# A two-stage attention and gated MLP kernel on one core: its beginning scheduled anew

## Chip, core and metric

One core of one Trainium2 chip runs one program. The metric is the device time of one execution in microseconds (us). The kernel before takes 796.01 us, the median of three runs (795.81 to 797.61).

## What is computed

```python
def _attn_ref(q, k, v, p):
    # sm_attn(a, b, c) = softmax(a @ b.T / 8) @ c, for each batch and head
    p_packed = sm_attn(p, k, v)
    return sm_attn(q, p_packed, p_packed)

def _moe_ref(x, w_gate, w_val, w_out, rms_g):
    rms = np.sqrt(np.mean(x * x, axis=-1, keepdims=True) + 1e-06)
    xn = x / rms * rms_g
    g = xn @ w_gate
    silu = g * (1.0 / (1.0 + np.exp(-g)))
    return silu * (xn @ w_val) @ w_out
```

There are 8 batches, 8 heads, 576 positions, 64 columns a head and 32 packed rows. x is the attention output laid out as 4608 tokens by 512; w_gate and w_val are 512 by 1536, w_out is 1536 by 512, all float32.

## The kernel before

**Two kinds of work.** Per batch b, `stage1` turns k, v and p into 32 packed rows a head (`pk_0x`, `pk_1x`, then transposed into `pts_0x`, ScalarE L831), and `packed_weights` multiplies these rows with the weights w_gate and w_val (L898, six column blocks c, eight products each), so that the MLP's first product is taken directly from the second attention's probabilities. Per unit u of 384 tokens, `query` and `attention` make the probabilities: scores (L1030), softmax (L1054 to L1064), transposition (L932), a product that gives the norm (L1099), its squares (L1107), the norm itself on GpSimd (L1124 to L1138), scaled probabilities (L1152), transposed again into `aTu`. `mlp` then runs 24 products of six multiplications (L1197, 12 column tiles ft for the gate and the value), each pair followed by `gated` (SiLU on ScalarE L1231, product with the value L1234, split into a high and a low half L1239 and L1245 into `hall`), and three output products of 36 multiplications each (L1222) whose results `store` writes out. There are 12 units. Everything is exact to about float32 by splitting into two float16 halves.

**The beginning.** Batch 0 and 1 and units 0 and 1 are done in a float32 way with transpositions on TensorE. In the beginning the weights are also made ready. `gv_piece(i)` loads one of 12 pieces of w_gate and w_val (1 MB each, alternately) into a raw room, turns it into a usable float32 form in `to_f32` (ScalarE L404, GpSimd L409, VectorE L411), squares it (ScalarE L459) and sums the squares over the rows on TensorE (L470). From each pair of pieces come scales: VectorE L481, then the small operations L345 to L350, L484, L486; GpSimd multiplies the w_val half by the ratio of the two scales (L489) and makes `gv_sc` and `wo_sc` (L492 to L494). `wo_piece(i)` loads and turns the six pieces of w_out in the same way (L404, L409, L411, squares L521); `wo_scale` waits for all six and makes one common scale (L538); `wo_split(i)` scales a piece (L554 on ScalarE or L557 on VectorE), writes its high half (ScalarE L559) and its low half (GpSimd L565). The raw rooms 0 to 3 lie in `ring`, 4 to 6 in `wo`, 7 and 8 in `hall`; a room is loaded again only once the piece in it has been turned, and `hall` can take results of `gated` only once the w_out pieces have left its rooms.

**What sets the order.** `Plan` is a list scheduler that runs while the program is built. Each job is a generator (a chain) that yields the engine, an estimated cost and the rooms or marks that it needs. `Plan.run` takes the step that can start first by the estimates; within a window (`CHOICE`, per engine) the step with the smallest rank (`RANK`) goes first. All engines then run the resulting fixed orders. All loads, stores and DMA transposes go through SyncE's one queue in that order. ScalarE needs one table for Exp and another for SiLU, and loads a table (ACT_TABLE_LOAD) whenever it goes from the one to the other.

Of the kernel before, what the change touches and what calls it, by code (L numbers as in the profile page):

```python
# [9 lines left out]
F32 = mybir.dt.float32  # L10
# [8 lines left out]
P = 128  # L19
# [14 lines left out]
LATENCY = {PE: 0.293, ACT: 0.16, EXP: 0.16, SILU: 0.16, DVE: 0.14, POOL: 0.1}  # L34
# [20 lines left out]
DVE_COST = (0.08, 1.04e-3)  # L55
# [17 lines left out]

class Plan:
# [36 lines left out]
    def go(self, chain, value=None):  # L111
        self.now, self.sent, self.chain = chain[2], chain[3], chain
        try:
            chain[4] = chain[0].send(value)
        except StopIteration:
            self.chains.remove(chain)
            return
        chain[2] = max(chain[2], self.now) if chain[4] is not None else self.now

    def settle(self):  # L120

        again = True
        while again:
            again = False
            for chain in sorted(self.chains, key=lambda c: (c[2], c[1])):
                ask = chain[4]
                if ask is None:
                    self.go(chain)
                elif isinstance(ask, Room):
# [15 lines left out]

    def start(self, chain):
        kind, _, *at = chain[4]
        e = ENGINE[kind]
        ready = at[0] if at and at[0] is not None else chain[3] if e == chain[5] and e in ("pe", "sp") else chain[2]
        if e == "pe" and chain[1] != NEVER:  # L150
            ready += SLACK[self.warm]
        return max(self.free[e], ready)

    def run(self):
        while self.chains:
            self.settle()
            steps = [c for c in self.chains if c[4] is not None and c[4][0] in ENGINE]
# [1175 lines left out]
```

## Time and profile before

| what | value |
|---|---|
| median of three runs | 796.01 us |
| the profiled execution, its own time | 796.5 us |
| its span, first to last instruction | 794.5 us |
| mean granted TensorE clock over the span | 0.967 |
| TensorE busy | 737.0 us (93%) |
| VectorE busy | 483.9 us (61%) |
| ScalarE busy | 472.2 us (59%) |
| GpSimd busy | 101.4 us (13%) |
| chain that ended last: TensorE's share | 78% |

Times within the trace count from the span's start. PE is TensorE, ACT ScalarE, DVE VectorE, POOL GpSimd, and SPq is SyncE's queue of DMA issues. PEclk is the granted TensorE clock as a share of 2.4 GHz: 0.50 is the level of 1.2 GHz, 1.00 that of 2.4 GHz. A matmul's end is modelled, so a busy PE is not a PE at its peak. A wait is named with the instruction that ended it.

### The profile page before, as it was taken

The numbers are of one execution on the slowest core, as the hardware profiler recorded it, in microseconds if no ns is written. First come the engines' busy times: TensorE is split into PE (matmuls) and PEld (weight loads), VectorE is DVE, ScalarE is ACT, GpSimd is POOL, SyncE is SP. The second block draws the span as 40 slices with busy tenths as digits, with TensorE's granted clock in tenths as the row PEclk, the third lists the DMA queues.
The fourth block names the chain that finished last, engine by engine and source line by source line (L and its number), as shares of the span: only waits on it lengthen the run. The fifth ranks groups of instructions, "written<-read, shape, count | busy, mean of one in ns | idle before, by whom it ended". The sixth has DMA issues, their size and how long they took to land.

```text
span 794.5 us, 17852 instructions
## 1 busy us (share of the span) xinstructions
PE 737.0 (93%) x7502; PEld 425.1 (54%) x7502; DVE 483.9 (61%) x985; ACT 472.2 (59%) x839; POOL 101.4 (13%) x144
## 2 busy tenths in 40 slices
PE   3676977799999999999999999999999999999998
PEld 2452543467544455478454555477455455676553
DVE  1768868487478447667578376476677465473341
ACT  1858877567658448658767457368677366271230
POOL 1666516101000000000001001000010000000000
PEclk9677989899999999999999999999999999999999
DMA  9994414343632732561636341734337212300001
GB/s 262 386 314 118 157 56 104 73 86 87 143 72 51 177 97 68 102 138 27 157 78 125 80 116 24 176 83 107 90 65 149 68 35 61 93 18 24 27 1 41
DMA packets 135504, 82.16 MB, mean 103 GB/s; under 512 B 98432, under 2 KB 123008, under 8 KB 135424
## 3 DMA queue, kind: packets, MB, share of 16 engines
q1 hardware_dynamic: 135424, 81.02, 42.0%
q8 instruction: 59, 0.97, 0.5%
q14 instruction: 21, 0.17, 0.1%
HBM read 47.97 MB, written 9.44 MB: 72 GB/s over the span
## 4 chain that ended last, share of the span: by engine, by line
PE 78%; ACT 7%; DVE 6%; DMA 5%; SPq 2%; issue 2%; POOL 1%; ACTq 0%; DVEq 0%; POOLq 0%
PE pm_2x L1222 11%; PE pm_1x L1222 10%; PE pm_2x L1197 8%; PE pm_1x L1197 8%; PE pm_0x L1222 8%; PE pm_3x L1197 7%; PE pm_0x L1197 7%; PE pm_3x L1222 6%; DMA hall<-in_moe_w_gate_dram 2%; PE pm_3x L898 2%; SPq L442 2%; PE quad L1037 1%; DMA big_3x<-in_k_dram 1%; PE pm_0x L898 1%; PE quad L793 1%
## 5 line engine op out<-in xcount | busy, mean ns | idle before, releaser
L1197 PEld LDWEIGHTS <-ring 128*128 128x128 f16 x2304 | 205.7, 98 | 107.0 <-issue 35.9
L1222 PEld LDWEIGHTS <-hall 128*128 128x128 f16 x1296 | 123.8, 99 | 153.0 <-issue 15.4
L1222 PE MATMUL pm_2x<-wo,hall 128*128 128x512 f16 x396 | 90.1, 379 | 0.0
L1222 PE MATMUL pm_1x<-wo,hall 128*128 128x512 f16 x360 | 81.8, 380 | 0.0
L1222 PE MATMUL pm_0x<-wo,hall 128*128 128x512 f16 x324 | 75.2, 382 | 3.3 <-POOL wo L565 3.3
L1239 ACT CAST hall<-t_1x 128x384 f16<-128x384 f32 x72 | 36.8, 510 | 34.9 <-DVE t_1x L1234 34.3
L1245 DVE TENSOR_TENSOR hall<-t_1x,hall 128x384 f16<-128x384 f32 x72 | 41.7, 579 | 17.2 <-ACT hall L1239 14.8
L1245 DVE TENSOR_TENSOR hall<-t_0x,hall 128x384 f16<-128x384 f32 x72 | 41.6, 578 | 14.9 <-ACT hall L1239 14.6
L1222 PE MATMUL pm_3x<-wo,hall 128*128 128x512 f16 x216 | 49.2, 383 | 0.0
L1239 ACT CAST hall<-t_0x 128x384 f16<-128x384 f32 x72 | 36.6, 508 | 17.1 <-DVE t_0x L1234 15.9
L1197 PE MATMUL pm_2x<-aTu_0x,ring 128*128 128x192 f16 (+1 forms) x324 | 45.6, 285 | 1.0 <-DVE ring L363 0.6
L1197 PE MATMUL pm_1x<-aTu_1x,ring 128*128 128x192 f16 (+1 forms) x324 | 45.8, 285 | 0.2 <-ACT t_0x L1231 0.2
L1197 PE MATMUL pm_3x<-aTu_1x,ring 128*128 128x192 f16 (+1 forms) x288 | 41.2, 286 | 3.1 <-DVE ring L363 1.7
L1197 PE MATMUL pm_1x<-aTu_0x,ring 128*128 128x192 f16 (+1 forms) x312 | 43.5, 283 | 0.2 <-ACT t_0x L1231 0.2
L1197 PE MATMUL pm_2x<-aTu_1x,ring 128*128 128x192 f16 (+1 forms) x288 | 41.3, 286 | 0.9 <-ACT hall L1239 0.7
L1197 PE MATMUL pm_0x<-aTu_0x,ring 128*128 128x384 f16 (+1 forms) x270 | 40.2, 291 | 0.7 <-ACT t_1x L1231 0.3
L1197 PE MATMUL pm_3x<-aTu_0x,ring 128*128 128x384 f16 (+1 forms) x246 | 37.6, 296 | 0.6 <-ACT t_1x L1231 0.5
L1197 PE MATMUL pm_0x<-aTu_1x,ring 128*128 128x384 f16 (+1 forms) x252 | 36.6, 288 | 0.0
L363 DVE SCALAR_TENSOR_TENSOR ring<-pm_3x,pw_sc,ring 128x512 f16<-128x512 f32 x31 | 23.1, 745 | 9.1 <-ACT ring L361 9.0
L361 ACT ACTIVATE ring<-pm_3x,pw_sc 128x512 f16<-128x512 f32 x31 | 21.1, 682 | 7.3 <-PE pm_0x L898 5.7
L1107 ACT ACTIVATE quad<-quad 128x512 f32<-128x512 f32 x36 | 21.1, 587 | 6.7 <-PE quad L1099 6.2
L363 DVE SCALAR_TENSOR_TENSOR ring<-pm_0x,pw_sc,ring 128x512 f16<-128x512 f32 x27 | 20.1, 746 | 7.8 <-ACT ring L361 7.4
(832 smaller groups left out, 1254.9 us busy)
## 6 DMA issues: line engine op xcount, KB each, us to landing
out_dram<-o_1x SPq DMA_DIRECT2D x18, 256.0 KB, 2.2
out_dram<-o_0x SPq DMA_DIRECT2D x18, 256.0 KB, 2.5
big_2x<-in_k_dram SPq DMA_DIRECT2D x6, 576.0 KB, 7.5
wo<-in_moe_w_gate_dram SPq DMA_DIRECT2D x3, 1024.0 KB, 14.3
wo<-in_moe_w_val_dram SPq DMA_DIRECT2D x3, 1024.0 KB, 10.8
ring<-in_moe_w_out_dram SPq DMA_DIRECT2D x3, 1024.0 KB, 5.5
hall<-in_moe_w_out_dram SPq DMA_DIRECT2D x3, 1024.0 KB, 5.0
big_0x<-in_v_dram SPq DMA_DIRECT2D x4, 576.0 KB, 6.3
```

Of the source, the lines that this page charges most:

```text
L361: nc.scalar.activation(hi, x, AF.Copy, scale=s)
L363: nc.vector.scalar_tensor_tensor(lo, x, s, hi, ALU.mult, ALU.subtract)
L442: nc.sync.dma_start(raw.rearrange("p k n e -> p k (n e)"), (w_gate, w_val)[n][:, 4 * c * P : 4 * (c + 1) * P].rearrange("(kt p) f -> p kt ...
L793: nc.tensor.matmul(pp[32 * j : 32 * j + 32, :D], a1T[:, c, 32 * j : 32 * j + 32], vf[:, j, cv, :], start=(c == 0), stop=(c == NCK - 1),)
L898: nc.tensor.matmul(ps[e][32 * j : 32 * j + 32, :], pg[h, j, :], wgv[h, c, j, :, :].rearrange("p w f -> p (w f)"), start=True, stop=True,)
L1037: nc.tensor.matmul(ps2[o : o + n, i, :, pi, :], qT[:, lq, i, pi, o : o + n], packs[b][3][:, lp, pi, :, :], start=(j == 0), stop=(j == 2),)
L1107: nc.scalar.activation(x, x, AF.Square, scale=2.0**-14, accum_out=ss[:, i : i + 1])
L1197: nc.tensor.matmul(psi[:, :, o : o + n], pw[:, g, lw, w, f * P : (f + 1) * P], aT[:, :, la, g, o : o + n], start=(j == 0), stop=(j == 5),)
L1222: nc.tensor.matmul(po, hall[:, ft, lh, ts], wo[:, ft, lw, :], start=(n == 0), stop=(n == 3 * NFT - 1))
L1239: nc.scalar.copy(hall[:, ft, 0, :], t)
L1245: nc.vector.tensor_tensor(hall[:, ft, 1, :], t, hall[:, ft, 0, :], ALU.subtract)
```

## The change

The scheduler gets two sets of constants: one (index 0) up to the point where unit 1's attention is planned to its end, one (index 1) after that. Ranks in the first set can depend on the number of the batch, unit or piece (`LATER`). Estimated costs change a little. A filler that could put dummy multiplications into idle time of TensorE is written, but its constants leave it out of the program. Then the steps themselves:

- the product of the w_val half with the scale ratio goes from GpSimd to ScalarE (column blocks 0 and 5 by the string `VAL_BY`'s letters A) and VectorE (D);
- the sums of squares go to another PSUM room, and each piece has its own maximum (12 short reductions in place of six longer ones);
- p of a batch is loaded ahead of its k; k of batch 1 waits for the issue of piece 9 in place of piece 11; w_out's pieces no longer wait for each other's issue;
- w_out's pieces use rooms 7, 8, 3, 8, 3, 8 in place of 8, 3, 8, 3, 8, 3;
- one more w_out scaling and one low half go to VectorE, some copies change between ScalarE and VectorE, and two low halves of unit 0 go to GpSimd.

```diff
-CHOICE = {'pe': 0.1, 'act': 0.335, 'dve': 0.324, 'pool': 0.378, 'sp': 0.437}
+CHOICE = ({'pe': 0.0, 'act': 0.281, 'dve': 0.275, 'pool': 0.352, 'sp': 0.398}, {'pe': 0.2, 'act': 0.36, 'dve': 0.338, 'pool': 0.208, 'sp': 0.269})
+IN_TURN = range(12)
+FILL = (0.6, 0.0, 0.0)
...
-RANK = {"scales": 0.1, "gated": 0.44, "pw_evict": 0.3, "store": 0.4, "attention": 0.63, "stage1": 0.6, "keys": 0.67, "v": 0.66, "query": 0.79, "pw": 0.8, "g": 0.9, "w": 1.0, "wo": 1.5, "wo_split": 1.65}
+RANK = ({"mlp": 1e9, "scales": 0.31, "gated": 0, "pw_evict": 0.39, "store": 0, "attention": 0.37, "stage1": 0.87, "keys": 0.49, "v": 0.21, "query": 0.79, "pw": 1.18, "g": 1.02, "w": 1.33, "wo": 1.34, "wo_split": 1.33}, {"mlp": 1e9, "scales": 0, "gated": 0.44, "pw_evict": 0.11, "store": 0.25, "attention": 0.71, "stage1": 0.6, "keys": 0.51, "v": 1.08, "query": 0.88, "pw": 1.56, "g": 1.6, "w": 1.13, "wo": 1.95, "wo_split": 1.52})
+LATER = {"attention": 0.08, "stage1": -0.24, "keys": 0.0, "query": 0.0, "pw": 0.17, "w": 0.04, "wo": 0.0, "wo_split": 0.04}
...
-WO_AT = (8, 3, 8, 3, 8, 3)
+WO_AT = (7, 8, 3, 8, 3, 8)
...
+VAL_BY = "DADDDA"
...
-WO_BY = "ADADAD"
-WO_LO = "PPPPPP"
-H_LO = "DDDDDDDDDDDD"
+WO_BY = "ADADDD"
+WO_LO = "PDPPPP"
+KEYS_AFTER = 9
+KEYS_BY = "ADAAAAADAADA"
+QUERY_BY = "ADDDAD"
+H_LO = "DDDPDDDDDDDP"
...
     def gv_piece(i):
...
-        if i:
-            yield "load", i - 1
+        if i and i in IN_TURN:
+            yield "issued", i - 1
...
-            pns[c] = yield Room("pm")
+            pn = yield Room("pa")
...
+        yield DVE, 0.4
+        nc.vector.tensor_reduce(mx[:, n : n + 1], pn[:, 2 * P :], AX.X, ALU.max)
...
-        yield POOL, pool(1024)
-        nc.gpsimd.tensor_scalar_mul(x, x, mx[:, 0:1])
+        if VAL_BY[c] == "A":
+            yield ACT, act(1024)
+            nc.scalar.activation(x, x, AF.Copy, scale=mx[:, 0:1])
+        elif VAL_BY[c] == "D":
+            yield DVE, 0.75
+            nc.vector.tensor_scalar_mul(x, x, mx[:, 0:1])
...
     def wo_piece(i):
...
-        yield ("load", 2 * NFC + i - 1)
+        if 2 * NFC + i in IN_TURN:
+            yield ("issued", 2 * NFC + i - 1)
...
     def keysets(b):
...
-        if b == 1:
-            yield ("load", 2 * NFC - 1)
+        if b == 1 and KEYS_AFTER:
+            yield ("issued", KEYS_AFTER)
...
+        pf = yield Room("pf")
+        for j in range(4):
+            yield LOAD, 16384
+            nc.sync.dma_start(pf[32 * j : 32 * j + 32], p[b, 2 * j : 2 * j + 2].rearrange("g r d -> r g d"))
+        t_p = plan.now
         kf0 = [None] * 2
...
     def gated(u, ft, pss, done):
...
-        if u == 0 and 8 in WO_AT and ft >= 5:
-            yield ("raw", 8, RAW_AT.count(8) + WO_AT.count(8))
+        if u == 0:
+
+            for k in (7,) if ft < 5 else (7, 8) if ft == 5 else (8,):
+                if k in WO_AT:
+                    yield ("raw", k, RAW_AT.count(k) + WO_AT.count(k))
```

What the scheduler makes of it is shown at three places. Line numbers of the change are those of its own file: L449 there is L404 of before, L507 is L459, L591 is L521, L857 is L766, L875 is L784, L1323 is L1231, L1338 is L1239, L1062 is L972, L1121 is L1030, L919 is L828, L988 is L898, L511 is L470, L700 is L610.

The first place is SyncE's queue behind the loads of q for unit 1. Before, k and p of batch 1 come next, then the fifth w_val piece:

```order
L959 DMA big_5x<-in_q_dram 64x8x192 x2
L576 DMA big_3x<-in_k_dram 96x4x384
L576 DMA big_0x<-in_k_dram 96x4x384
L599 DMA pf_0x<-in_p_dram 32x2x64 x4
L442 DMA wo_77<-in_moe_w_val_dram 128x4x512
L506 DMA ring<-in_moe_w_out_dram 128x2x1024
```

With the change:

```order
L1049 DMA big_5x<-in_q_dram 64x8x192 x2
L576 DMA ring<-in_moe_w_out_dram 128x2x1024
L489 DMA wo_79<-in_moe_w_val_dram 128x4x512
L682 DMA pf_0x<-in_p_dram 32x2x64 x4
L664 DMA big_3x<-in_k_dram 96x4x384
L664 DMA big_0x<-in_k_dram 96x4x384
```

A piece of w_out and the fifth w_val piece now stand ahead of p and k of batch 1, and p ahead of k. (At the queue's start p of batch 0 likewise stands ahead of its k.)

The second place is TensorE between the transposition of batch 0's packed rows (L828, with the change L919) and the scores of unit 0 (L1030, with the change L1121). Before, transpositions of unit 1's q (L972), one piece's sums (L470) and the transposition of batch 1's p (L610) stand between:

```order
L828 MATMUL quad<-ident_66,pk_1x 64x128
L972 MATMUL pm_0x<-ident_66,big_5x 64x128 x8
L972 MATMUL pm_1x<-ident_66,big_5x 64x128 x8
...
L470 MATMUL pm_2x<-o_1x,onesb 128x256
L610 MATMUL pm_3x<-ident_66,pf_0x 64x128 x4
L972 MATMUL pm_0x<-ident_66,big_5x 64x128 x8
L1030 MATMUL quad<-pb_0_85,big_4x 128x2x32 x12
```

With the change:

```order
L908 MATMUL quad<-tiny_0x,ones 128x1 x2
L919 MATMUL quad<-ident_66,pk_0x 64x128
L919 MATMUL quad<-ident_66,pk_1x 64x128
L1121 MATMUL quad<-pb_0_87,big_4x 128x2x32 x12
L988 MATMUL pm_1x<-wgv,pg_0x 32x512
```

The scores now follow at once, and what stood between comes after the first block of packed weights (L988).

The third place is ScalarE around its first SiLU. Before, the first softmax of batch 1 (L766) is followed by the table for SiLU, and the second comes in the middle of unit 0's SiLUs, behind a table load of its own; these rows are those around that second softmax:

```order
L1231 ACTIVATE t_0x<-pm_0x,usc_0x 128x384
L404 ACTIVATE wo_77<-hall 128x1024
L766 ACT_TABLE_LOAD
L766 ACTIVATE a_0x,tiny_43x<-quad,tiny_42x,qk_74 128x576
L1239 CAST hall<-t_1x 128x384
...
L521 ACTIVATE o_0x,wo_ss<-wo_77 128x1024
L1231 ACT_TABLE_LOAD
L1231 ACTIVATE t_1x<-pm_3x,usc_0x 128x384
```

With the change, before the first SiLU:

```order
L857 ACTIVATE a_0x,tiny_36x<-quad,tiny_35x,qk_76 128x576
L591 ACTIVATE o_1x,wo_ss<-wo_79 128x1024
L875 COPY a1T_0x<-quad 96x768
L591 ACTIVATE o_0x,wo_ss<-wo_79 128x1024
L552 ACTIVATE wgv<-wgv,tiny_33x 128x4x256
L896 ACTIVATE junk_0x,tiny_31x<-pk_2x 128x64
L449 ACTIVATE wo_79<-hall 128x1024
L857 ACTIVATE a_0x,tiny_43x<-quad,tiny_42x,qk_76 128x576
L1323 ACT_TABLE_LOAD
L1323 ACTIVATE t_0x<-pm_0x,usc_0x 128x384
```

Between the copy of unit 0's scaled probabilities (L940, with the change L1030) and the first SiLU stand now both softmaxes of batch 1, four conversions and three squares of w_out pieces, one square of a w_val piece and one ratio product (L552). No table load is left among unit 0's SiLUs.

## Rows read from the trace of the kernel before

**Rows 1.** Busy time by stretch: stretch, its length, busy time of each engine (instructions), PEclk, DMA

```profile
0.00:45.95 45.95, 23.30 (x252) 15.84 (x253) 21.79 (x52) 22.68 (x32) 23.08 (x32) 0.77 1.02 313
45.95:82.00 36.05, 25.73 (x293) 16.02 (x293) 27.06 (x53) 24.99 (x39) 24.27 (x26) 0.78 0.62 197
...
88.66:122.15 33.49, 28.94 (x258) 16.48 (x256) 23.70 (x49) 28.77 (x51) 6.25 (x5) 0.90 0.29 95
122.15:143.76 21.61, 12.82 (x112) 5.04 (x112) 17.38 (x24) 15.15 (x23) 13.23 (x8) 0.94 0.37 94
143.76:165.00 21.24, 21.24 (x266) 11.70 (x267) 9.71 (x25) 10.65 (x20) 1.96 (x5) 0.90 0.37 69
165.00:740.00 575.00, 567.89 (x6000) 330.75 (x5999) 360.56 (x748) 352.37 (x644) 27.90 (x62) 1.00 0.41 90
```

**Rows 2.** Timeline of the first 46 us: start, length, engine, line, what [idle before <-what ended it]

```profile
2.93 2.12 SPq L599 DMA_DIRECT2D pf_0x<-in_p_dram  x4
...
13.76 1.13 PE L610 MATMUL pm_0x<-ident,pf_0x 128*64 128x128 f32 x8 [13.76 <-DMA pf_0x<-in_p_dram]
...
15.64 1.98 PE L972 MATMUL pm_1x<-ident,wgv 128*64 128x128 f32 x16
...
22.14 0.72 PE L738 MATMUL quad<-wgv,pT_0x 64*32 64x288 f32 x16
...
45.95 0.37 ACT L831 ACTIVATE pts_0x<-quad,tiny_20x 128x128 f32<-128x128 f32 x1 [0.67 <-PE quad L828]
```

**Rows 3.** The chain of waits, its first piece

```profile
2.20 10.53 DMA big_3x<-in_k_dram
```

**Rows 4.** Instructions by line and form up to 145 us, ScalarE: busy us, mean ns | idle before

```profile
L404 ACT ACTIVATE wgv<-wo 128x1024 f32<-128x1024 f32 x6 | 6.8, 1132 | 2.1 <-DMA wo<-in_moe_w_val_dram 2.1
L459 ACT ACTIVATE o_0x<-wgv 128x1024 bf16<-128x1024 f32 x6 | 6.3, 1057 | 3.5 <-DVE wgv L411 3.5
L1231 ACT ACT_TABLE_LOAD x2 | 2.6, 1283 | 0.0
```

**Rows 5.** Timeline, 45 to 85 us: GpSimd's ratio, TensorE, the last w_val piece, the scaled probabilities

```profile
45.63 3.90 POOL L489 TENSOR_SCALAR wgv<-wgv,tiny_17x 128x1024 f32<-128x1024 f32 x1
...
51.30 0.66 PE L610 MATMUL pm_3x<-ident,pf_0x 128*64 128x128 f32 x8 [1.45 <-DMA pf_0x<-in_p_dram]
...
52.77 2.89 PE L1030 MATMUL quad<-pb,big_4x 128*128 128x64 f32 x24
...
61.47 1.15 POOL L409 TENSOR_SCALAR wo<-wo 128x1024 uint32<-128x1024 uint8 x1 [1.66 <-DMA wo<-in_moe_w_val_dram]
...
76.76 1.31 ACT L1152 ACTIVATE e_0x<-e_0x,trio_3x 128x256 f32<-128x256 f32 x3 [0.20 <-POOL trio_3x L1138]
...
84.84 1.14 PE L1197 MATMUL pm_0x<-aTu_0x,ring 128*128 128x384 f16 x6 [0.21 <-DVE ring L363]
```

**Rows 6.** Timeline, VectorE's scaling of a w_out piece, alone and beside GpSimd's low halves

```profile
120.59 0.75 DVE L557 TENSOR_SCALAR big_2x<-wo,wo_sc 128x1024 f32<-128x1024 f32 x1
...
133.08 2.62 DVE L557 TENSOR_SCALAR big_0x<-wo,wo_sc 128x1024 f32<-128x1024 f32 x1
```

**Rows 7.** Timeline, ScalarE and TensorE from the first SiLU on

```profile
88.66 0.58 ACT L1231 ACTIVATE t_0x<-pm_0x,usc_0x 128x384 f32<-128x384 f32 x1
...
122.15 0.56 ACT L1231 ACTIVATE t_1x<-pm_3x,usc_0x 128x384 f32<-128x384 f32 x1
...
135.74 1.04 ACT L559 CAST wo<-big_0x 128x1024 f16<-128x1024 f32 x1 [4.19 <-DVE big_0x L557]
...
143.76 1.51 PE L932 MATMUL quad<-ident,e_0x 128*128 128x128 f32 x6 [4.13 <-DVE e_0x L1064]
...
146.34 3.47 PE L1222 MATMUL pm_3x<-wo,hall 128*128 128x512 f16 x12
```

**Rows 8.** The chain of waits, one output product of 36 multiplications

```profile
320.47 7.77 PE pm_1x L1222 x36
```

**Rows 9.** DMA issues up to 160 us: KB each, median us to landing

```profile
hall<-in_moe_w_out_dram SPq DMA_DIRECT2D x3, 1024.0 KB, 5.0
```

**Rows 10.** Timeline, one later attention: its DMA transposition and its first use

```profile
304.90 1.43 SPq L1077 DMA_TRANSPOSE aT_0x<-hl_0x  x1
...
309.08 0.21 PE L1099 MATMUL quad<-pav_0x,aT_0x 32*64 32x64 f16 x1
```

More of the change, by code (lines that the diff above doesn't have):

```diff
@@ L71, with __init__ @@
     pass
+class Chain:
+    def __init__(self, gen, key, t):
+        self.gen, self.key = gen, key
+        self.end = self.sent = t
+        self.since = 0.0
+        self.ask = self.engine = None
 class Plan:
     def __init__(self):
+        self.rooms = {}
         self.now = self.sent = 0.0
@@ L152, in start, with fill @@
-        return max(self.free[e], ready)
-    def run(self):
+        if at and at[0] is not None:
+            base = at[0]
+        else:
+            base = chain.sent if e == chain.engine and e in ("pe", "sp") else chain.end
+        ready = max(base, chain.since)
+        t = float(ready)
+        if e == "pe" and chain.key[0] != "mlp":
+            t += SLACK[self.stage]
+        return max(self.free[e], t), ready
+    def fill(self, until, matmul):
+        begin = self.free["pe"]
+        n = int(FILL[1] * (until - begin) / 0.11)
+        for name in ("pa", "psc", "pm"):
+            spare = [r for r in self.rooms[name] if r[0] <= begin]
+            if spare:
+                break
+        if until - begin < FILL[0] or until > FILL[2] or not spare or not n:
+            return
+        self.rooms[name].remove(spare[0])
+        for _ in range(n):
+            matmul(spare[0][1])
+        self.free["pe"] += 0.11 * n
+        self.rooms[name].append((self.free["pe"], spare[0][1]))
@@ L162, in run @@
-            for n, c in enumerate(steps):
-                t = self.start(c)
-                t -= AGE * max(0.0, t - c[2])
-                if c[4][0] in (EXP, SILU) and c[4][0] != self.table:
-                    t += TABLE
-                starts[n] = t
-            first = min(starts, key=lambda n: (starts[n], steps[n][1]))
-            e = ENGINE[steps[first][4][0]]
-            near = [n for n in starts if ENGINE[steps[n][4][0]] == e and starts[n] <= starts[first] + CHOICE[e]]
-            chain = steps[min(near, key=lambda n: (steps[n][1], starts[n]))]
@@ L172, in run @@
-            t, (kind, cost, *_) = self.start(chain), chain[4]
-            e = ENGINE[kind]
+            starts = []
+            for c in steps:
+                t, ready = self.start(c)
+                t -= AGE[self.stage] * max(0.0, t - ready)
+                if c.ask[0] in (EXP, SILU) and c.ask[0] != self.table:
+                    t += TABLE
+                starts.append((t, self.precedence(c), c))
+            first = min(starts, key=lambda s: s[:2])
+            e = ENGINE[first[2].ask[0]]
@@ L174, in run @@
+            window = CHOICE[self.stage][e]
+            chain = min(
+                (s for s in starts if ENGINE[s[2].ask[0]] == e and s[0] <= first[0] + window), key=lambda s: (s[1], s[0])
+            )[2]
+            t, ready = self.start(chain)
+            kind, cost, *_ = chain.ask
+            if e == "pe":
+                self.fill(t, matmul)
+                t = max(t, self.free["pe"])
             if kind == LOAD:
```

303 lines of the change are left out of this document (170 added, 133 removed).

## The prediction

> **What bounds the kernel now.** I read the busy time by stretch first, then the timeline of the beginning, then the chain of waits. From 165 to 740 us TensorE is busy for 567.9 of 575 us at a granted clock of 1.00 [rows 1]: that part is TensorE's own work, and the change leaves the number of multiplications as it is. Up to 143.76 us it is otherwise: no engine is full, and TensorE waits. It does nothing until 13.76, because p lands last [rows 2]; it makes its first MLP product at 84.84 [rows 5]; from 122.15 to 143.76 it is busy for 12.8 of 21.6 us [rows 1]. From 143.76 on it hardly stops. So the time is, to a few us, the moment at which TensorE becomes dense, plus a remainder that stays. The engine to follow up to there is ScalarE: 25.0 of 36.1 us, then 28.8 of 33.5 us, the fullest of all in the MLP's first unit [rows 1].
>
> The profiled execution took 796.5 us (span 794.5 and 2.0 around it), 0.5 above the median of 796.0.
>
> **The change, milestone by milestone.**
>
> *Batch 0's packed rows (ScalarE L831, 45.95 before).* The second half of k lands at 2.20 + 10.53 = 12.73 [rows 3]; p, whose four issues come behind it (2.93 to 5.05), lands at 13.76, and TensorE's queue begins with p [rows 2]. With p first, p waits for nothing and k, held back by 64 KB, lands near 13.0. Then k's transpositions end near 15; the first group of unit 0's q stands next, can start as now when q is there (15.64 [rows 2]) and takes 1.1 to 2 us; the scores L738 follow near 16.8 in place of 22.14: 5.3 earlier, because the other q groups now stand behind them. From L738 to L831 it is 23.8 us. Twelve conversions and squares stand on ScalarE between the steps of this chain, ten with the change, 1.13 or 1.06 each [rows 4]: 2.2 less, and 0.8 for waits on pieces that have landed by then. So 16.8 + 20.8 = 37.6; ends 36 and 41.
>
> *First MLP product (84.84 before).* From L831 to the copy of unit 0's final probabilities ScalarE works 25.0 of 36.1 us [rows 1]; in the new order a conversion, a square and a ratio product are added (1.13 + 1.06 + 1.13, the last priced by L404, same shape and engine [rows 4]): 28.3 us. Two waits go: unit 0's scores stood behind batch 1's p, which landed at 51.30 (L1030 at 52.77), and GpSimd's ratio, 3.90 us at 45.63, stood ahead of the packed rows' product with rms_g [rows 5]. What is late next is the last w_val piece: the DMA engines are full up to 46 us (share 1.02 [rows 1]) and carry the same bytes, so it lands at about 61.5 as before (L409 at 61.47 [rows 5]), and its conversion now stands ahead of the probabilities' last scaling L1152. From L1152 to the first product it is 84.84 - 76.76 = 8.1 us [rows 5]: 61.5 + 1.1 + 0.4 + 8.1 = 71 at the least. With ScalarE as badly filled as before (69%) it is 37.6 + 28.3 / 0.69 = 78.6. I take 73, nearer the low end, since two of the old waits are gone; the copy ends at 71.
>
> *First SiLU (88.66 before [rows 7]).* Here the gain is given back. ScalarE now has four conversions (4.5), four squares (4.2), a ratio product (1.1), the table load (1.28 [rows 4]) and six instructions of 512 to 768 columns, at 0.85 between SiLU's 0.58 for 384 [rows 7] and L404's 1.13 for 1024: 5.1. That is 16.2 us: 71 + 16 = 87. The fourth w_out piece, loaded when the second has left its room and 5.0 us on the way [rows 9], is due near the same moment. TensorE has four PSUM buffers, so it makes four products and waits.
>
> *Last SiLU of unit 0 (122.15 before).* Out go two table loads (2.6), two conversions, two squares, a scaling, one exponential and one copy, about 10.7; in come six high halves of w_out (1.04 each [rows 7]) and six evictions of packed weights (about 0.7), with small ones 11.5. So 28.8 + 0.8 = 29.6 us, and with the same filling (86%) 34.4: 87 + 34.4 = 121.4.
>
> *TensorE dense (143.76 before).* Before, the high and low halves of w_out come behind the last SiLU: ScalarE waits 4.19 us for VectorE's scaling, and TensorE 4.13 for unit 1's softmax [rows 7]. Now the high halves stand ahead. After the last SiLU come the product, the halves, a table load and the softmax, about 7 us, beside 36 output multiplications of 7.77 us [rows 8]: 121.4 + 7.8 = 129.2. GpSimd's last low halves have to end inside it.
>
> **VectorE beside GpSimd.** Four ratio products and one more scaling go to VectorE. The same form took 0.75 us alone and 2.62 beside GpSimd's low halves [rows 6]. I take 0.75: GpSimd's long ratios are gone, and its conversions leave it free between pieces. 0.75 each is 3.0 us on VectorE, busy 27.1 of 36.1 us [rows 1]; 2.62 each would be 10.5. The Trainium skill, page "SBUF — State Buffer", section "Who interferes with whom", says that a VectorE instruction in a two-port mode and GpSimd lock each other out for a whole instruction, whoever starts first; by that the move only changes who waits, and the sum would be up to 7.5 us less of a gain.
>
> **The sum.** 143.76 - 129.2 = 14.6. There TensorE has done 36 output multiplications of unit 0, before 33: 3 x 7.77 / 36 = 0.65 more. From 143.76 to 165 the clock was 0.90 on average [rows 1], after an idle stretch: 4.2 us at the lower of its two levels (twelve multiplications took 3.47 us [rows 7], at full rate 2.6), worth 2.1; now TensorE comes in without that pause. Together 17.4: 796.5 - 17.4 = 779.1, against the median 778.6. **Forecast: 779 us.** The second set of constants I cost at nothing, plus or minus 3: all 42 later blocks of packed weights still stand at least 42 multiplications ahead of their first use, as all but one did before, and TensorE has 7.1 us of idle to lose in 575 [rows 1].
>
> **Rivals.**
> - *Fuller.* ScalarE filled to 97% from the first SiLU, and the first SiLU 3 us earlier: 772. For it: fewer table loads and no load to wait for. Against: nowhere in the beginning is an engine that full.
> - *Given back.* The unit's products start after a pause of TensorE, so at half clock, and ScalarE is filled to 75%: 29.6 / 0.75 = 39.5; GpSimd's low halves end 4 us later: 779 + 5 + 4 = 788. For it: clock 0.90 in that unit already [rows 1].
> - *Lock.* Each of the four ratio products costs 2.62, all on the path: 779 + 7.5 = 786.5. For it: [rows 6]. Against: there GpSimd was busy without a gap. The skill's rule above would make it so.
> - *Slower.* In the later units the product L1099 stands earlier in TensorE's row: by 12, 36, 30 and 36 multiplications of 384 columns in units 2, 3, 6 and 9, by 36, 24 and 12 of half that width in 4, 7 and 10. At 7.77 / 36 x 384 / 512 = 0.162 us [rows 8] that is 18.5 + 5.8 = 24.3 us. If the transpositions it waits for come no earlier, TensorE waits all of it: 803. It is slower than before from 17.4 of 24.3, 72%. For it: this product is only just in time now, issued 304.90, used 309.08 [rows 10]. Against: the softmax ahead of it has moved up too.
> - *No effect.* With full DMA engines and each piece already loaded in turn, the order of loads brings nothing, and ScalarE's waits only change places: 795.
>
> **Chances.** Forecast 0.53 (own range 775 to 784), fuller 0.12, given back 0.17, lock 0.07, slower 0.07, no effect 0.04. What this kernel's measurement can tell from no change is 0.3%, 2.4 us. Faster: the first four, less a tail, 0.88; same 0.04; slower 0.08. The range takes in fuller, lock and given back: 771 to 790; outside stay slower, no effect and small tails.
>
> **What would show it.** The changed kernel's first MLP product near 73, first SiLU near 87, last one near 121, unit 1's transposition L932 near 129, with no wait of over 1 us on unit 1's softmax; TensorE from 165 us on with no more idle than now. Wrong would be: a first SiLU behind 92 (then the w_out loads or the order on ScalarE hold it), VectorE's ratio products at over 2 us, or waits of several us ahead of L1099 in later units.

## The result and the profile after

The changed kernel takes **800.93 us** (median of 9 runs, 797.96 to 801.82), the kernel before 796.16 on the same chip (9 runs, 795.06 to 798.23): ratio 1.0048, 95% interval 1.0031 to 1.0065. It is slower by half a per cent, where 779 and a gain were forecast. The profiled execution is the one of 800.93, span 799.2; that of before has 796.5 and 794.5. One of the later executions, with p alone moved, ran at a granted clock of 0.744 and took 966.05 us; it is left out of that run's time and ratio.

| Event (unit 0 unless named) | before | predicted | after |
|---|---|---|---|
| scores of batch 0, TensorE L829 | 22.14 | 16.8 | 17.67 |
| packed rows of batch 0, ScalarE L922 | 45.95 | 37.6 | 41.42 |
| copy of the final probabilities ends, ScalarE L1030 | 82.0 | 71 | 80.4 |
| first MLP product, TensorE L1289 | 84.84 | 73 | 82.29 |
| first SiLU, ScalarE L1323 | 88.66 | 87 | 96.37 |
| last SiLU | 122.15 | 121.4 | 136.74 |
| unit 1's transposition, TensorE L1022 | 143.76 | 129.2 | 146.66 |
| from there to the end of the span | 650.7 | 648.0 | 652.5 |

These are the rows of the timeline of the changed kernel (start, length, engine, line, what [idle before <- what ended it]); they answer to [rows 2, 5, 7].

```profile
17.67 0.72 PE L829 MATMUL quad<-wgv,pT_0x 64*32 64x288 f32 x16
...
37.86 1.04 PE L511 MATMUL quad<-o_0x,onesb 128*128 128x256 bf16 x4 [0.81 <-DVE pk_1x L892]
...
38.93 0.42 DVE L535 TENSOR_REDUCE tiny_14x<-quad 128x1 f32<-128x256 f32 x1 [1.13 <-PE quad L511]
...
41.42 0.37 ACT L922 ACTIVATE pts_0x<-quad,tiny_15x 128x128 f32<-128x128 f32 x1 [2.22 <-PE quad L919]
...
51.05 0.94 ACT L1150 ACTIVATE e_0x<-e_0x,tiny_18x 128x768 f32<-128x768 f32 x1 [2.80 <-DVE e_0x L1147]
...
56.02 0.85 PE L1022 MATMUL quad<-ident,e_0x 128*128 128x128 f32 x6 [2.59 <-DVE tiny_19x L535]
...
65.46 0.27 PE L1190 MATMUL quad<-pav_0x,aT_0x 32*128 32x64 f16 x12
...
66.88 2.17 DVE L456 SCALAR_TENSOR_TENSOR wgv<-wgv,wo 128x1024 uint32<-128x1024 uint32 x1
...
69.14 1.06 ACT L507 ACTIVATE o_0x<-wgv 128x1024 bf16<-128x1024 f32 x1 [2.31 <-DVE wgv L456]
70.11 0.58 ACT L1198 ACTIVATE quad<-quad 128x512 f32<-128x512 f32 x1
...
79.64 0.79 ACT L1030 ACTIVATE aTu_0x<-quad 128x768 f16<-128x768 f32 x1
...
82.29 1.20 PE L1289 MATMUL pm_0x<-aTu_0x,ring 128*128 128x384 f16 x6
...
96.37 0.58 ACT L1323 ACTIVATE t_0x<-pm_0x,usc_0x 128x384 f32<-128x384 f32 x1
...
136.23 1.34 PE L1289 MATMUL pm_2x<-aTu_0x,ring 128*128 128x384 f16 x6 [3.61 <-DVE ring L416]
137.37 9.45 PE L1314 MATMUL pm_3x<-wo,hall 128*128 128x512 f16 x36
...
146.66 0.82 PE L1022 MATMUL quad<-ident,e_0x 128*128 128x128 f32 x6
```

The scores come 4.5 us earlier and so do the packed rows. Unit 0's exponential is still 6.6 us ahead of before's (57.68). Then the lead melts: the transposition of the probabilities waits 2.59 us for VectorE's reduction of a weight's column sums, the product L1190 comes 9 us behind that transposition, and its squares L1198 stand behind a square of a weight piece that waits for VectorE. At the copy L1030 1.6 us are left, and from the first SiLU on the kernel is behind.

The busy time by stretch, to be read beside [rows 1] (length, busy time of each engine with its instructions, TensorE's granted clock, DMA share, GB/s):

```profile
45.95:82.00 36.05, 25.52 (x287) 15.10 (x287) 29.67 (x58) 25.34 (x38) 16.81 (x26) 0.78 0.80 233
...
122.00:143.76 21.76, 14.44 (x66) 6.74 (x60) 19.64 (x25) 15.37 (x22) 12.08 (x8) 0.84 0.40 97
143.76:165.00 21.24, 21.24 (x263) 11.37 (x261) 9.90 (x22) 12.20 (x22) 2.17 (x5) 1.00 0.43 91
165.00:740.00 575.00, 564.64 (x5999) 328.40 (x5995) 358.02 (x746) 347.30 (x638) 26.71 (x62) 1.00 0.41 89
```

VectorE is busy for 19.64 of the 21.76 us up to 143.76, the fullest engine there; ScalarE is not. The clock behind 143.76 is 1.00 in place of 0.90. From 165 to 740 TensorE is idle 3.3 us longer than before.

What fills VectorE at the end of unit 0 is in the timeline of VectorE, GpSimd and ScalarE:

```profile
121.64 2.19 DVE L641 TENSOR_SCALAR big_1x<-wo,wo_sc 128x1024 f32<-128x1024 f32 x1
...
126.21 0.74 DVE L416 SCALAR_TENSOR_TENSOR ring<-pm_1x,pw_sc,ring 128x512 f16<-128x512 f32 x1
...
127.53 1.83 DVE L650 TENSOR_TENSOR wo<-big_1x,wo 128x1024 f16<-128x1024 f32 x1
...
129.80 0.27 DVE L710 TENSOR_REDUCE tiny_52x<-pf_0x 128x2 f32<-128x128 f32 x1
130.11 1.26 DVE L407 TENSOR_SCALAR tiny_50x<-tiny_52x 128x2 uint32<-128x2 uint32 x1
131.40 2.05 DVE L408 TENSOR_SCALAR tiny_50x<-tiny_50x 128x2 f32<-128x2 f32 x1
133.48 2.04 DVE L409 TENSOR_SCALAR tiny_51x<-tiny_50x 128x2 uint32<-128x2 uint32 x1
...
128.23 3.11 POOL L653 TENSOR_TENSOR wo<-big_4x,wo 128x1024 f16<-128x1024 f32 x1
131.30 2.12 POOL L653 TENSOR_TENSOR wo<-big_3x,wo 128x1024 f16<-128x1024 f32 x1
133.38 2.12 POOL L653 TENSOR_TENSOR wo<-big_2x,wo 128x1024 f16<-128x1024 f32 x1
...
135.56 0.35 ACT L414 ACTIVATE pd_0x<-pf_0x,tiny_51x 128x64 f16<-128x64 f32 x1 [4.21 <-DVE tiny_51x L409]
136.74 0.58 ACT L1323 ACTIVATE t_1x<-pm_1x,usc_0x 128x384 f32<-128x384 f32 x1 [0.83 <-DVE hall L1344]
```

L407 to L409 are three instructions on two columns, the scale of batch 2's p. Its load is issued at 97.08 us here, ahead of k's; before, it was issued at 133.49, behind k's, and the same three instructions stood behind GpSimd's last low half and took 0.17 us each. These are rows of the kernel before:

```profile
136.86 2.13 POOL L565 TENSOR_TENSOR wo<-big_0x,wo 128x1024 f16<-128x1024 f32 x1 [1.71 <-ACT wo L559]
...
144.05 0.17 DVE L355 TENSOR_SCALAR tiny_53x<-tiny_53x 128x2 f32<-128x2 f32 x1
```

In the changed kernel each of the three ends within 0.03 us of the end of the low half L653 beside it (131.37 and 131.34, 133.45 and 133.42, 135.52 and 135.50): the second and third last about as long as one of GpSimd's instructions, the first as long as was left of one. ScalarE waits 4.21 us for their result, and the unit's last SiLU stands behind that wait in its queue. TensorE, which waited 3.61 us for VectorE's eviction of a packed-weight product (L416), then does its next 36 output multiplications in 9.45 us in place of 7.77 [rows 8]; its granted clock from 136.74 to 146.66 was 0.83.

### The profile page after: what moved, and what is told of

It is laid out like the page before. It is cut to its first block, busy times and chain, and to the rows that moved or that the text cites. A ratio compares the mean times of both kernels' runs of the same rounds, so it can differ in the third digit from the quotient of the medians.

```text
span 799.2 us, 17847 instructions
## 1 busy us (share of the span) xinstructions
PE 738.2 (92%) x7502; PEld 424.9 (53%) x7502; DVE 484.6 (61%) x994; ACT 468.1 (59%) x835; POOL 84.7 (11%) x140
## 4 chain that ended last, share of the span: by engine, by line
PE 73%; DVE 11%; DMA 6%; ACT 5%; issue 3%; SPq 1%; DVEq 0%; ACTq 0%
PE pm_0x L1314 9%; PE pm_3x L1314 8%; PE pm_2x L1289 8%; PE pm_0x L1289 8%; PE pm_2x L1314 7%; PE pm_1x L1289 7%; PE pm_3x L1289 7%; PE pm_1x L1314 6%; PE quad L1128 1%; DVE ring L416 1%; PE pm_2x L988 1%; PE quad L1190 1%; DMA big_2x<-big_0x 1%; DMA big_4x<-in_q_dram 1%; DVE wgv L456 1%
## 5 line engine op out<-in xcount | busy, mean ns | idle before, releaser
L1289 PEld LDWEIGHTS <-ring 128*128 128x128 f16 x2304 | 205.3, 98 | 116.6 <-issue 45.2
L1314 PE MATMUL pm_3x<-wo,hall 128*128 128x512 f16 x360 | 83.3, 384 | 0.0
L1314 PE MATMUL pm_0x<-wo,hall 128*128 128x512 f16 x360 | 81.9, 379 | 0.0
L1314 PE MATMUL pm_2x<-wo,hall 128*128 128x512 f16 x288 | 66.3, 379 | 0.0
L1314 PE MATMUL pm_1x<-wo,hall 128*128 128x512 f16 x288 | 65.3, 379 | 0.0
L1338 ACT CAST hall<-t_1x 128x384 f16<-128x384 f32 x72 | 36.7, 510 | 33.4 <-DVE t_1x L1326 33.1
L1289 PE MATMUL pm_1x<-aTu_0x,ring 128*128 128x384 f16 (+1 forms) x300 | 44.9, 293 | 4.9 <-DVE ring L416 3.7
L1289 PE MATMUL pm_2x<-aTu_0x,ring 128*128 128x384 f16 (+1 forms) x318 | 46.0, 288 | 3.7 <-DVE ring L416 3.6
L1338 ACT CAST hall<-t_0x 128x384 f16<-128x384 f32 x72 | 36.6, 509 | 20.6 <-DVE t_0x L1326 20.0
L1289 PE MATMUL pm_2x<-aTu_1x,ring 128*128 128x192 f16 (+1 forms) x330 | 46.9, 285 | 0.9 <-ACT t_0x L1323 0.6
L1289 PE MATMUL pm_0x<-aTu_0x,ring 128*128 128x192 f16 (+1 forms) x288 | 41.1, 287 | 1.6 <-ACT t_0x L1323 1.2
L1289 PE MATMUL pm_0x<-aTu_1x,ring 128*128 128x192 f16 (+1 forms) x300 | 41.2, 281 | 1.1 <-ACT t_1x L1323 0.8
L1289 PE MATMUL pm_1x<-aTu_1x,ring 128*128 128x192 f16 (+1 forms) x288 | 40.1, 283 | 0.3 <-DVE t_0x L1326 0.3
L1289 PE MATMUL pm_3x<-aTu_0x,ring 128*128 128x384 f16 (+1 forms) x246 | 36.6, 293 | 0.0
L1289 PE MATMUL pm_3x<-aTu_1x,ring 128*128 128x384 f16 (+1 forms) x234 | 36.5, 297 | 0.0
L1198 ACT ACTIVATE quad<-quad 128x512 f32<-128x512 f32 x36 | 21.1, 587 | 7.4 <-PE quad L1190 7.0
L416 DVE SCALAR_TENSOR_TENSOR ring<-pm_3x,pw_sc,ring 128x512 f16<-128x512 f32 x29 | 21.6, 744 | 4.5 <-ACT ring L414 4.2
L416 DVE SCALAR_TENSOR_TENSOR ring<-pm_1x,pw_sc,ring 128x512 f16<-128x512 f32 x26 | 19.4, 744 | 5.9 <-ACT ring L414 5.8
```

The lines of the kernel that those rows point to most:

```text
L416: nc.vector.scalar_tensor_tensor(lo, x, s, hi, ALU.mult, ALU.subtract)
L1198: nc.scalar.activation(x, x, AF.Square, scale=2.0**-14, accum_out=ss[:, i : i + 1])
L1289: nc.tensor.matmul(psi[:, :, o : o + n], pw[:, g, lw, w, f * P : (f + 1) * P], aT[:, :, la, g, o : o + n], start=(j == 0), stop=(j == 5),)
L1314: nc.tensor.matmul(po, hall[:, ft, lh, ts], wo[:, ft, lw, :], start=(n == 0), stop=(n == 3 * NFT - 1))
L1338: nc.scalar.copy(hall[:, ft, 0, :], t)
```

## The experiments

All expectations were written before the runs; ratios are to the kernel before, measured beside each. A dense point is the start of unit 1's transposition; what follows it is the rest.

**Batch 2's p held.** In `keysets`, ahead of the conversion of p:

```diff
+            if b == 2:
+                for i in range(NFC):
+                    yield ("wo_hl", i)
+                t_p = plan.now
             yield DVE, 1.0, t_p
```

> The changed kernel, with one wait of the scheduler more: the conversion of batch 2's p to halves (small VectorE and ScalarE instructions) is placed only after w_out's high and low halves. Theory (three of this chain's VectorE instructions, 0.17 us each alone, took 1.26, 2.05 and 2.04 beside GpSimd's low halves, and ScalarE stood 4.21 us for them with SiLUs behind): unit 0's last SiLU moves from 136.7 to about 133, unit 1's transposition from about 146.8 to 143, the time to about 797.5. Rival (the low halves themselves, which end at 135.5, or VectorE's other work beside them set the end, and the chain only filled a wait): last SiLU behind 135.5, time within 1 us of 801.

795.11 us, ratio 0.9971 (0.9952 to 0.9991): 0.77% less than the changed kernel, 6 us. The theory holds; the gain is larger than expected, the last SiLU's as forecast. From the first SiLU to the last it is 36.0 us (97.97 to 133.96) in place of 40.4. The profiled execution (797.54) lies above the median; it has the dense point 4.2 us earlier and the rest 0.8 longer (653.3), so the trace shows less of the gain than the medians. The timeline has the same instructions behind the low halves; the first of them stood beside another GpSimd instruction and ended with it (137.41 and 137.40):

```profile
133.96 0.58 ACT L1327 ACTIVATE t_1x<-pm_1x,usc_0x 128x384 f32<-128x384 f32 x1 [1.91 <-PE pm_1x L1293]
...
136.25 1.15 POOL L1345 TENSOR_TENSOR hall<-t_1x,hall 128x384 f16<-128x384 f32 x1
...
136.85 0.56 DVE L407 TENSOR_SCALAR tiny_50x<-tiny_52x 128x2 uint32<-128x2 uint32 x1
137.45 0.17 DVE L408 TENSOR_SCALAR tiny_50x<-tiny_50x 128x2 f32<-128x2 f32 x1
137.65 0.17 DVE L409 TENSOR_SCALAR tiny_51x<-tiny_50x 128x2 uint32<-128x2 uint32 x1
...
142.50 0.82 PE L1026 MATMUL quad<-ident,e_0x 128*128 128x128 f32 x6
```

**Low halves by VectorE as well:** `WO_LO = "DDDDDD"` on top of it.

> As p2_held, and all six low halves of w_out by VectorE instead of five by GpSimd and one by VectorE. Theory (VectorE and GpSimd hold each other up in this stretch): VectorE's instructions on SBUF take their single times (scaling 0.75, no instruction over 1.4 us from 117 to 140), the last SiLU comes at 131 to 133, the time is 1 to 3 us under p2_held's. Rival (VectorE, busy 10.00 of 10 us from 120 to 130, is simply full): five more subtractions of 1.0 to 1.3 us, 5 to 6.5 us, stand ahead of the last SiLUs' work on VectorE, the time is that of p2_held or up to 3 us more.

795.11 us, 0.9965 (0.9946 to 0.9983): the rival's time, but by the theory's mechanism.

```profile
121.13 0.74 DVE L641 TENSOR_SCALAR big_1x<-wo,wo_sc 128x1024 f32<-128x1024 f32 x1
...
125.57 1.21 DVE L650 TENSOR_TENSOR wo<-big_0x,wo 128x1024 f16<-128x1024 f32 x1
...
130.82 0.58 ACT L1327 ACTIVATE t_1x<-pm_1x,usc_0x 128x384 f32<-128x384 f32 x1 [1.00 <-PE pm_1x L1293]
...
139.36 0.82 PE L1026 MATMUL quad<-ident,e_0x 128*128 128x128 f32 x6
```

From 117 to 140 us no VectorE instruction takes over 1.22 us; the last SiLU comes 34.9 us behind the first (95.90), near the prediction's 34.4. The dense point is 3.1 us earlier, the medians are equal; the two profiled spans differ by 2.5. What the runs can tell is that it is no loss.

**The same edit in the kernel before**, `WO_LO` alone:

> The kernel before with one edit: the six low halves of w_out by VectorE in place of GpSimd; TensorE's order is the same but for three output multiplications. Theory (VectorE and GpSimd hold each other up wherever both work on SBUF alone, in the kernel before too: VectorE's scaling took 2.62 in place of 0.75 there, its casts of batch 1's rows 2.15 and 1.39, and TensorE waited 4.13 us for unit 1's softmax): unit 1's transposition at 138 to 140 in place of 143.8, the low halves 1.21 us each, time 791 to 793. Rival (VectorE takes 6 x 1.21 = 7.3 us more, as much as it is held up now): 796 within 1.5.

793.68 us, 0.9952 (0.9930 to 0.9974): the move is worth 3.8 us in the kernel before too, and the stretched rows are gone (the first of these two took 2.15 us before, the second 2.62 [rows 6]):

```profile
127.64 0.28 DVE L363 SCALAR_TENSOR_TENSOR pav_2x<-pk_2x,tiny_47x,pav_2x 128x64 f16<-128x64 f32 x1
...
131.08 0.74 DVE L557 TENSOR_SCALAR big_0x<-wo,wo_sc 128x1024 f32<-128x1024 f32 x1
```

The forecast of the dense point missed: it is at 144.41. In part this execution's beginning was later throughout (scores at 23.01, last SiLU at 123.85); but from the last SiLU on, too, only 1.05 us are won up to the dense point. Six more output multiplications are done by then (39 in place of 33), and the rest is 647.7 in place of 650.7, with a granted clock of 1.00 up to 165 us in place of 0.90. So most of the gain lies behind the dense point, which the theory did not say.

**The ratio back on GpSimd:** `VAL_BY = "PPPPPP"` in the changed kernel.

> The changed kernel with w_val's six ratio products back on GpSimd; all else stays (the scheduler places the neighbours anew). Theory (VectorE was busy 9.8 of 10 us from 50 to 70, and four ratio products of 0.75 are 3.0 of them; GpSimd's take 3.9 each and lock VectorE meanwhile): no gain, the copy of unit 0's final probabilities at 80 to 84 in place of 79.6, the time 801 to 805. Rival (the ratio's move to VectorE is what held the first stage up): the copy at 75 to 77, the time 797 to 799.

806.88 us, 1.0120 (1.0092 to 1.0147): 5.7 us more than the changed kernel, the copy at 83.78. In this order the ratio's move is no cause of the loss. On VectorE each product took 0.75 us.

**Parts of the change alone, in the kernel before.** p ahead of k for batch 0 and the ratio by `"DADDDA"` together; then each by itself:

```diff
-        yield POOL, pool(1024)
-        nc.gpsimd.tensor_scalar_mul(x, x, mx[:, 0:1])
+        if "DADDDA"[c] == "A":
+            yield ACT, act(1024)
+            nc.scalar.activation(x, x, AF.Copy, scale=mx[:, 0:1])
+        else:
+            yield DVE, 0.75
+            nc.vector.tensor_scalar_mul(x, x, mx[:, 0:1])
```

> The kernel before with two parts of the change alone: p ahead of k for batch 0, and the ratio products of w_val by VectorE (four) and ScalarE (two). Constants, loads and w_out's rooms stay. Theory (these two parts carry the gain at the front, and the loss came with the rest of the new order, above all batch 2's p beside the low halves): unit 1's transposition at 139 to 141 in place of 143.8, time 792 to 794. Rival (the scheduler of before fills the time gained with other work as the changed one does): 796 within 1.5.

> The kernel before with p ahead of k for batch 0 alone. Theory (the scores of batch 0 come 2.5 us earlier and the packed rows with them, but GpSimd's ratio of 3.90 us still stands ahead of the packed rows' product with rms_g and locks VectorE): a third to a half of before_p_first_ratio's gain, 794 to 795. Rival (the whole gain comes from p): 792.5.

> The kernel before with the ratio products alone moved from GpSimd to VectorE (four) and ScalarE (two). Theory (this is the part that pays: back on GpSimd it cost the changed kernel some 6 us): 793 to 794. Rival (without p ahead, the stage waits for the packed rows of batch 0 anyway): 796 within 1.5.

Together 792.54 us, 0.9945 (0.9926 to 0.9964), dense point 141.01; p alone 791.96, 0.9922 (0.9893 to 0.9952), dense point 140.72; the ratio alone 797.54, 0.9999 (0.9978 to 1.0021). The pair goes by the theory, the single parts by the rivals: within these intervals p gives all of it. With the ratio alone, packed rows came at 51.40 in place of 45.95 and the first SiLU at 96.49. The order explains at least part of it: the transposition of unit 1's q now stood ahead of that of batch 0's packed rows in TensorE's queue, and TensorE waited 3.66 us for that q's load (until 47.79). So this run prices the new order together with the engine's change, not the change of engine by itself.

The pair has the same work left at its dense point as the changed kernel (36 output multiplications done in both). So the two can be laid side by side: the dense points differ by 146.66 - 141.01 = 5.65 us, the rests by 652.54 - 649.09 = 3.45.

**The two that pay, added up:**

> As before_p_first_ratio (792.5), and the six low halves by VectorE. Theory (the gain at the front and the one at the end of unit 0 add up): unit 1's transposition at 136 to 138, time 787 to 790. Rival (the two overlap, since the last SiLUs wait for w_out's scale, which comes from its last piece's load at 104 us either way): 792 within 1.5.

> The kernel before with p ahead of k for batch 0 and the six low halves of w_out by VectorE, the ratio left on GpSimd. Theory (the two gains measured alone, 0.78% and 0.48%, lie at two ends of the beginning and add up, and the ratio's move brings nothing): 787 to 789. Rival (the ratio's move matters once p is first): 791 or more, as before_p_ratio_low_dve or worse.

790.91 us, 0.9910 (0.9882 to 0.9938), dense point 139.75, and 790.73, 0.9928 (0.9903 to 0.9953), dense point 139.44. Both are faster than either kernel, and both theories missed: the first time lies in its rival's range, the second between theory and rival. By the medians the two gains add up in part only: 0.78 and 0.48% would make 1.26, and 0.7 to 0.9 were measured. The intervals are 0.2 to 0.3% to either side and overlap, so how much is lost, and the ratio's share beside p, stay undecided.

**The order in the front.** The squares of the last four weight pieces held until the attention's squares are placed, and (a run of its own, on top of p2_held_low_dve) the column sums back in the rooms pm:

```diff
+            if i >= 8:
+                yield "squares", 0
             sq0 = yield Room("o")
```

```diff
-            pn = yield Room("pa")
+            pn = yield Room("pm")
```

> The changed kernel, with one wait of the scheduler more: ScalarE's squares of the last four w_gate and w_val pieces are placed only after the squares of unit 0's attention (L1198), which in the changed kernel stood behind such a square that waited 2.31 us for VectorE. Theory (the order on ScalarE between unit 0's softmax and its scaled copy gives the first gain back): unit 0's scaled squares at about 66.5 in place of 70.1, the copy of its final probabilities at 75 to 77 in place of 79.6, the time 2 to 4 us under 800.9. Rival (behind that copy ScalarE has 16 us of work up to the first SiLU anyway, and what is put off there comes back): copy earlier, first SiLU still at 95 to 97, time within 1.5 us of 801.

> As p2_held_low_dve, and the column sums of the weights' squares go to the four rooms pm again, as before, in place of the two rooms pa that the attention's own products need. Theory (with the sums in pa, unit 0's attention waits for VectorE's reductions of them: 2.59 us ahead of its transposition at 56.0, and its product came 4.9 us after its probabilities were there): the squares of unit 0's attention at 62 to 66 in place of 70.1, the copy of its final probabilities at 72 to 76 in place of 79.6, time 2 to 4 us under 795.1. Rival (the sums then hold up the packed weights and the transpositions of q and k, which use pm): time the same as p2_held_low_dve within 1.5 or longer.

Squares first: 798.50 us, 1.0002 (0.9981 to 1.0024), 0.46% under the changed kernel. The amount is the theory's, the way is neither's: the squares came at 68.23, the copy at 79.59 as before the edit, but the first SiLU at 87.19, because batch 1's second softmax, three squares of w_out pieces, a conversion and a ratio product now stood behind it. Sums in pm: 798.88, 1.0024 (1.0005 to 1.0044), slower than p2_held_low_dve, though the front did what the theory said and more:

```profile
38.38 0.37 ACT L926 ACTIVATE pts_0x<-quad,tiny_15x 128x128 f32<-128x128 f32 x1 [1.09 <-PE quad L923]
...
59.07 0.58 ACT L1202 ACTIVATE quad<-quad 128x512 f32<-128x512 f32 x1
...
73.07 0.79 ACT L1034 ACTIVATE aTu_0x<-quad 128x768 f16<-128x768 f32 x1
...
117.01 0.58 ACT L1327 ACTIVATE t_1x<-pm_2x,usc_0x 128x384 f32<-128x384 f32 x1
...
130.02 0.37 ACT L926 ACTIVATE pts_0x<-quad,tiny_50x 128x128 f32<-128x128 f32 x1 [1.34 <-PE quad L923]
...
141.48 0.82 PE L1026 MATMUL quad<-ident,e_0x 128*128 128x128 f32 x6
```

The copy ends at 73.86 and the last SiLU comes at 117.01, near where the prediction had wanted them or earlier (71 and 121.4), and still the dense point is at 141.48, 2.1 us later than in p2_held_low_dve. Unit 1 needs batch 1's packed rows; in the changed kernel they were there at 109.95, here at 130.02, put off behind unit 0's SiLUs. While TensorE waits for unit 1 it goes ahead with unit 0: 78 output multiplications are done at the dense point in place of 36, at 7.77 us for 36 [rows 8] some 9.1 us of work. That lead is lost behind it. The rest is 657.0 us against 653.9, and from 141.48 to 785 TensorE is idle for 20.4 us against 11.2, in units early and late; which order there does it is not shown. So the sums in pa do hold the front up by some 6 us at the copy (79.34 to 73.07), and a faster unit 0 by itself bought nothing here: unit 1's chain set the dense point, and the later units lost what was won as work.

**The constants and the rooms.** The second set replaced by before's; before's scheduler with the second set from unit 1 on; the first set replaced by before's; `SLACK = (0.306, 1.0)`, a margin of the scheduler, on p2_held_low_dve; w_out's old rooms (`WO_AT`):

> The changed kernel, with the kernel before's ranks and windows (RANK, CHOICE) as the second of the two sets, which holds from unit 1 on; the first set and all else stay. Up to the end of unit 0 the order is the changed one. Theory (the second set costs some 3 us in the later units, where TensorE was busy 564.6 of the 575 us from 165 to 740 against 567.9 before): about 798, TensorE again near 568 there, and the two single waits of 3.6 us ahead of MLP products gone. Rival (the later units lose by what the first stage leaves them, p ahead of k or the order in which packed weights enter, whatever the ranks): 801, TensorE near 565 as now.

> The kernel before with the changed kernel's second set of ranks and windows from unit 1 on; the beginning keeps its own order up to there. Theory (the second set itself makes the later units longer, by the 3.4 us that the changed kernel's rest, 652.5 us from unit 1's transposition on, has over 649.1 with before's set and the same work left): 798 to 800, TensorE idle from 200 to 300 us over 3. Rival (the set is not at fault, but how it fits what the scheduler assumes of costs and what the beginning leaves it): 796 within 1.5, or a change of over 6 us in either direction.

> The changed kernel with the kernel before's ranks and windows as the first of the two sets; the second set, the rooms, p and the ratio stay. Theory (the new first set puts packed weights and batch 1's rows ahead of unit 0's attention, and batch 2's p ahead of the last SiLUs, so it gives the front's gain back): 793 to 797, the copy of unit 0's final probabilities under 78. Rival (the old ranks do the same with the new rooms, since the sums in pa hold the attention either way): 799 to 803.

> As p2_held_low_dve, and the second value of SLACK, the margin by which the scheduler places TensorE's steps other than MLP products late, 1.0 in place of 0.3. Theory (the later units lose some 4 us against before by short waits of 0.4 to 1.2 us where an attention's step stands right behind what it waits for, in unit 2 from 233 to 239 us above all): TensorE idle from 200 to 300 us 1 to 2 in place of 4.4, time 2 to 3 us under 795.1. Rival (the margin moves the attention later, and products of the next unit wait for it instead): 795 or more.

> The changed kernel with w_out's six pieces in the rooms of before. Theory (the rooms decide only when the first piece is loaded; w_out's scale waits for the last piece, converted at 102.0 in the changed kernel and 104.2 before): time within 2 us of 800.9, w_out's scale within 2 us of 117.7. Rival (the early piece's 1 MB in the full queues ahead of the last w_val pieces holds up the front): 2 to 4 us faster.

820.52 us, 1.0285 (1.0257 to 1.0312); 816.67, 1.0244 (1.0218 to 1.0269); 810.11, 1.0158 (1.0134 to 1.0182), the copy at 89.12; 817.38, 1.0248 (1.0219 to 1.0277); 801.98, 1.0063 (1.0042 to 1.0084). The first four theories fall, and the fifth is right in the time alone. The single waits of 3.6 us that the first of these expectations put into the later units lie at 127.0 and 136.2 us, at the end of unit 0. Each set of ranks in the other's surroundings costs 18 to 20 us in the rest (672.5 in place of 652.5; 668.6 in place of 650.7): a set is fitted to the costs that the scheduler assumes and to what the beginning leaves, and can't be priced apart from them. The rooms are worth nothing either way, though w_out's scale came at 113.65 with the old ones and not within 2 us of 117.7.

## Why the prediction was wrong

*What bounds.* The reading that the dense point sets the time, and that the rest stays, carried for the larger part: of the whole miss of 21.8 us (800.93 against 779.1) 17.5 are in the dense point and 4.5 in the rest (the profiled execution has 0.2 less around its span). It is no rule: with the sums in pm the rest moved more than the dense point.

*Scores and packed rows.* The scores were right to 0.9. From there to the rows it took 23.75 us, as before (23.8); the 3.0 us taken off for two conversions and for waits did not come. ScalarE was busy for 14.8 us of that stretch in place of 18.15, and the stretch was as long, so ScalarE's work did not set it. The chain of waits there runs through four sums L511 of 1.0 us on TensorE and VectorE's reductions L535 of 0.42 us that free their rooms in pa; with the sums back in pm the stretch took 20.6 us (17.79 to 38.38), as forecast (20.8), where the same kernel with them in pa took 23.8. **Taking ScalarE's work for the limit failed, and the time of the rows with it, by 3.8.**

*First MLP product.* The working set two different moments side by side: the low end, 71, was for the product, the high end, 37.6 + 28.3 / 0.69 = 78.6, is for the end of the copy, 2.8 us earlier. For the copy the high end was nearly right: with rows 3.8 us late it gives 82.4, and 80.4 was measured, ScalarE busy for 27.7 of the 39.0 us (71%). I chose the low end because two waits were gone. What I left out stands in the diff: the sums moved from pm to pa, which the attention's products need. **This choice failed, by another 5.6 to the copy.** With the sums in pm it is 35.5 us from the rows to the copy's end in place of 39.0; 33.4 were forecast, so some 2 us stay without a cause.

*First SiLU.* 16 us behind the copy: 15.9 measured, ScalarE busy for 14.6 of them. Right.

*Last SiLU.* 34.4 us forecast, 40.4 measured. The work was right, ScalarE busy for 29.4 us against 29.6; the filling was not, 73% against 86%, for ScalarE stood behind VectorE (4.21 us at a time). **This is the mechanism that I missed.** I had the row [rows 6] and the Trainium skill's rule beside it, but asked it only of the ratio products. These took 0.75 each on VectorE; it was the rows newly placed beside the low halves that locked. Over their single times (0.74, 1.21, three times 0.17) the scaling, the subtraction and the chain of batch 2's p took 1.45 + 0.62 + 4.84 = 6.9 us more. With the chain held back the stretch was 36.0 and the time 6 us less; with the low halves off GpSimd too it was 34.9. **The filling of 86% failed, by 6.0 us: it had VectorE's work beside the low halves at its single times.**

*Dense.* Behind the last SiLU 7.8 us were forecast, 9.9 measured, 1.7 of them on the 36 multiplications after TensorE's pause. The clock's 2.1 us behind the dense point came (1.00 in place of 0.90), but not because TensorE had no pause: its pause of 3.61 us lay ahead of the dense point now, and the 1.7 us are the price of the lower clock there (0.83 over 9.92 us, so 3.4 us at the lower level).

*Second set.* Costed at nothing plus or minus 3; the rest is 4.5 us longer than forecast, 3.45 against the same work in before's order. The wait I had as the rival "slower", L1190 behind its DMA transposition, was there twice on TensorE, 0.98 and 0.85 us in place of 24.3. The timeline of unit 2 shows the kind:

```profile
233.55 0.27 PE L1190 MATMUL quad<-pav_0x,aT_0x 32*128 32x64 f16 x12 [0.98 <-DMA aT_0x<-hl_0x]
...
238.17 0.16 PE L1221 MATMUL quad<-ru_1x,onesb 128*128 128x3 bf16 x1 [1.23 <-POOL ru_1x L1217]
238.92 1.30 PE L1289 MATMUL pm_1x<-aTu_0x,ring 128*128 128x384 f16 x5 [0.59 <-ACT t_1x L1323]
```

TensorE's steps stand there right behind what they wait for. That this comes from the set rather than from its fit to the rest stays open, as the runs on the constants say.

*Rivals and chances.* "Slower" had the right sign for a wrong reason, and a chance of 0.07; "lock" had the right mechanism in the wrong place. "Given back" had nearly the right filling (75%) behind the first SiLU, but set it beside a lower clock of TensorE; from the first SiLU to the last that clock was 0.88, against 0.90 before. All the milestones I summed were of one chain; no rival asked what else the new order puts beside GpSimd's long instructions.

## What to carry to other kernels

When an order is changed, go through what now stands beside long GpSimd instructions on SBUF, the small VectorE instructions above all, and through what stands behind each of them on every queue: holding back three of 0.17 us gave 6. Look in the diff for each buffer that changes its pool, and name who else takes from that pool. And when one chain is made faster, find the next unit's chain and where the scheduler has put it, before the gain is booked. A run that moves one step also moves its neighbours when a scheduler places them: read the new order before the price is put down to the step.

## What was not expected of the hardware

VectorE instructions on two columns took 1.26, 2.05 and 2.04 us against 0.17 alone: each ended within 0.03 us of GpSimd's instruction of 1024 columns beside it (3.11, 2.12 and 2.12 us), so the cost was what was left of GpSimd's, not their own size. GpSimd waited as well, 3.11 in place of 2.12, where VectorE's subtraction L650 had begun 0.70 us earlier. In the same stretch VectorE's eviction from PSUM kept its 0.74 and its reduction its 0.27. The Trainium skill, page "SBUF — State Buffer", section "Who interferes with whom", says that the lock is for a whole instruction, whoever is first, and that reductions never take part; the rows agree. No run here tells which of an instruction's operands or modes decides.
